# Gated attention feeding a rotation layer: fewer full-float32 chunks, gate sums as matrix products, and a re-planned order

## The chip, the cores and the metric

One NeuronCore of one Trainium2 chip runs the whole kernel. The metric is the device time of one execution in microseconds (us). Lower is better.

## The reference

The inputs are q, k, v and a gate logit, each of 4 batches x 8 heads x 768 tokens x 48, and four weight matrices. What is computed, cut to its core:

```python
f = 1 / (1 + exp(-f_logit))
for t in range(768):
    state = f[t][:, None] * state + outer(k[t], v[t])
    y[t] = q[t] @ state
x = heads side by side                       # 4 x 768 x 384
theta = x @ w_theta
zr, zi = x * cos(theta), x * sin(theta)
u = x + w_tok_r @ zr + w_tok_i @ zi          # over the 768 tokens
out = u + maximum(u @ w_ch, 0)
```

All of it is float32. In this case `w_theta` and `w_tok_i` are drawn about 5.5 times larger than the usual scale, so the angles are large.

## The kernel before, in words

**Chunks.** Each batch is cut into 6 chunks of 128 tokens, 24 chunks in all, numbered m. The recurrence is done chunk by chunk. `gate_clamp` (line 267) bounds the logits below, `gate_open` (271) forms log(1 + exp(-f)) by two ScalarE (ACT) activations, `gate_sum` (277) forms the running sum over the tokens of the chunk as one VectorE (DVE) scan, `gate_exp` (281) takes the exponential of the sum and of its negative, and `gate_q` and `gate_k` (292, 296) multiply q and k with these. `att_scores`, `att_keys`, `att_state`, `att_old` and `att_out` (324 to 402) are the TensorE (PE) products of linear attention within the chunk and with the state, `att_mask`, `att_mid`, `att_new` and `att_fade` their DVE or GpSimd (POOL) steps, and `att_turn` (408) transposes the chunk of x.

**The rotation layer.** `angles` (436) multiplies the chunk with `w_theta`; `whole`, `settle`, `fold` and `trig` reduce the angle and take sine and cosine; `rotate` (468) makes the two products zr and zi. `products` (487) then adds one chunk's share of the token mixing to one block of the output in PSUM: 144 such pieces, named f0, f1 and f2 by the block of 128 channels, 36 for each batch. `channel` (511) is the product with `w_ch`, 3 calls for each half of a batch, and `finish` and `store` end it.

**Two forms of product.** The chunks of batch 0 (`FULL = 1`, in batches) use float32 operands as they are: a piece is two float32 products, and PE runs each as two instructions. All other chunks use operands split in two float32r parts, a high one and a rest, and a piece is six float32r products. The splits are steps of their own: `split_xh`, `split_xl`, `split_zh`, `split_zl` (427 to 482) for the data, `split_hi` and `split_lo` (239, 245) for the weights. The weights arrive as 64-bit numbers in 16 parts and are first decoded (`decode_low`, `decode_high`, `decode_join`, 212 to 226).

**The order.** `ORDER` (72) is one hand-fixed list of steps for all engines. Each step name stands for the next call of its function (`lf` loads the next chunk of f, `gs` is the next `gate_sum`, `sc` the next `att_scores`, `ke` the next transposes of k, and so on); a suffix /D, /P or /A moves the step to DVE, POOL or ACT. Every engine runs its own steps in the order of the list, and each queue is in order, the SP queue that issues all DMAs too. `PLACES` (55) names the buffer that each tile takes. PSUM has two double banks ("a") and four single banks ("b", `bank`, 309) for everything else.

Of the kernel before, what the change touches and what calls it, by code (L numbers as in the profile page):

```python
# [8 lines left out]
F32 = mybir.dt.float32  # L9
# [9 lines left out]
DM = H * D  # L19
# [17 lines left out]
F_MIN = -44.0  # L37
# [6 lines left out]
FULL = 1  # L44
# [3 lines left out]
CUT = 0  # L48
# [7 lines left out]
    "a": "0110110101001010110101010101010101010101010101010",  # L56
    "b": ("012301230120123023300300002121123222230230203120310202001031023333312312023011203100000023"
        "1030303030032123123211120303031"),
    "f": "012012012012012012012012",
# [8 lines left out]
    "wp": "0123456789abcdefghijklmno013245687cd",  # L68
    "x": "012012012012012012012012",
    "z": "0123450123412342342350421350421350421",  # L70
}
ORDER = (
# [39 lines left out]
@with_exitstack  # L112
def gla_moe_kernel(
    ctx: ExitStack,
    tc: tile.TileContext,
    q: bass.AP,
    k: bass.AP,
    f: bass.AP,
    v: bass.AP,
    vt: bass.AP,  # L120
    w_theta: bass.AP,
    w_r: bass.AP,
    w_i: bass.AP,
    w_ch: bass.AP,
# [614 lines left out]
```

## Time and profile before

| what | value |
|---|---|
| time, median of 3 runs | 337.95 us (337.77 to 339.97) |
| the profiled execution | 338.16 us, span 335.5 us |
| PE busy | 316.8 us, 94% of the span |
| DVE busy | 243.4 us, 73% |
| ACT busy | 192.9 us, 58% |
| POOL busy | 112.3 us, 33% |
| table loads on ACT | 22 of 1.28 us |

The span runs from the first to the last instruction that the profiler saw; 2.66 us of the profiled execution lie around it. Busy shares are averages over stages with different limits, so the stages have to be read one by one.

### The profile page before, as it was taken

How to read it: one execution, taken by the hardware profiler on the slowest of the kernel's cores; microseconds unless marked ns; L12 is line 12 of the kernel's file. 1: busy time of each engine (PE TensorE's matmuls, PEld its weight loads, DVE VectorE, ACT ScalarE, POOL GpSimd, SP SyncE). 2: the span in 40 equal slices, each digit the busy share in tenths (PEclk: the TensorE clock that was granted, in tenths of full speed). 3: DMA queues.
4: the chain of work that ended last, by engine and by line, in shares of the span. 5: the costliest groups of instructions: out<-in, count | busy, mean ns of one | idle time of the engine just before them, and what ended most of it. 6: DMA issues, size and time to landing. Idle time of an engine off the chain costs nothing.

```text
span 335.5 us, 9996 instructions
## 1 busy us (share of the span) xinstructions
PE 316.8 (94%) x4320; PEld 280.7 (84%) x4320; DVE 243.4 (73%) x394; ACT 192.9 (58%) x321; POOL 112.3 (33%) x109
## 2 busy tenths in 40 slices
PE   0798999999999999999999999999999999999993
PEld 0685676567676789999999999999999999999992
DVE  5999999999999899968659777774526677441031
ACT  6789977787696799847468253953805342310010
POOL 2452074318100146265371248143800521103110
PEclk9999999999999999999999999999999999999998
DMA  7989779758660463240405353250122102000022
GB/s 266 395 244 304 254 249 340 249 181 308 243 212 17 150 225 111 91 156 15 130 3 168 115 160 117 88 178 0 33 73 79 49 2 73 0 2 0 0 73 77
DMA packets 21619, 45.54 MB, mean 136 GB/s; under 512 B 2369, under 2 KB 5441, under 8 KB 21569
## 3 DMA queue, kind: packets, MB, share of 16 engines
q1 hardware_dynamic: 21568, 44.84, 39.6%
q8 instruction: 36, 0.59, 0.7%
q14 instruction: 15, 0.11, 0.1%
HBM read 40.11 MB, written 4.72 MB: 134 GB/s over the span
## 4 chain that ended last, share of the span: by engine, by line
PE 83%; DVE 9%; ACT 2%; DMA 2%; issue 2%; DVEq 0%; ACTq 0%
PE pm L498 47%; PE pch L516 10%; PE pth L442 9%; PE wide L401 4%; PE wide L393 3%; PE wide L333 3%; PE pxt L411 2%; PE psk L347 2%; PE wide L362 2%; DVE f L279 2%; DMA out_dram<-ut 1%; DVE z L475 1%; DVE raw L215 1%; DMA f<-in_f_dram 1%; DVE k L299 1%
## 5 line engine op out<-in xcount | busy, mean ns | idle before, releaser
L498 PE MATMUL pm<-wp,z 128*128 128x384 f32 x648 | 117.1, 336 | 0.0
L498 PEld LDWEIGHTS pm<-wp,z 128*128 128x128 f32 x648 | 112.4, 188 | 0.0
L498 PE MATMUL pm<-value,z 128*128 128x384 f32 x144 | 49.3, 487 | 0.2 <-DVE z L475 0.2
L516 PE MATMUL pch<-uhl,wch 128*128 128x384 f32 x216 | 40.2, 339 | 0.4 <-DVE ut L176 0.4
L498 PEld LDWEIGHTS pm<-value,z 128*128 128x128 f32 x144 | 26.3, 190 | 15.9 <-DVE value L226 0.5
L516 PEld LDWEIGHTS pch<-uhl,wch 128*128 128x128 f32 x216 | 37.5, 188 | 1.0 <-DVE ut L176 0.7
L290 POOL COPY pes<-p 128x4 f32<-128x4 f32 x24 | 11.4, 476 | 72.6 <-ACT p L286 68.2
L502 DVE TENSOR_TENSOR ut<-pm,ut 128x384 f32<-128x384 f32 x24 | 13.1, 552 | 29.8 <-PE pm L498 29.8
L176 ACT CAST uhl<-ut 128x384 fp32r<-128x384 f32 x18 | 9.2, 509 | 41.5 <-DVE ut L502 41.5
L279 DVE TENSOR_TENSOR_SCAN f<-carry,f 128x512 f32<-128x512 f32 x24 | 29.1, 1222 | 0.7 <-ACT f L275 0.7
L433 POOL TENSOR_TENSOR xl<-ut,xh 128x384 fp32r<-128x384 f32 x13 | 13.5, 1041 | 46.1 <-DVE xh L176 29.1
L286 ACT ACTIVATE p<-f 128x512 f32<-128x512 f32 x24 | 15.1, 628 | 21.7 <-DVE f L279 21.3
L509 POOL TENSOR_TENSOR uhl<-ut,uhl 128x384 fp32r<-128x384 f32 x13 | 13.5, 1047 | 37.0 <-DVE uhl L176 18.6
L347 PE MATMUL psk<-ident,k 128*128 128x128 f32 (+1 forms) x96 | 16.8, 302 | 8.9 <-DVE k L299 8.8
L269 POOL TENSOR_SCALAR f<-f 128x512 f32<-128x512 f32 x14 | 23.3, 1668 | 1.5 <-DMA f<-in_f_dram 1.5
L530 DVE SCALAR_TENSOR_TENSOR ut<-pch,ut 128x384 f32<-128x384 f32 x24 | 13.0, 553 | 14.7 <-PE pch L516 14.4
L482 POOL TENSOR_TENSOR z<-w,z 128x768 fp32r<-128x768 f32 x9 | 17.4, 1931 | 17.8 <-ACT z L176 9.6
L442 PE MATMUL pth<-wth,xh 128*128 128x384 f32 x108 | 23.0, 348 | 0.0
L299 DVE SCALAR_TENSOR_TENSOR k<-f,k 128x512 f32<-128x512 f32 x24 | 19.5, 813 | 3.7 <-ACT f L287 3.6
L401 PEld LDWEIGHTS wide<-v,sc 64*64 64x64 f32 x768 | 15.0, 140 | 8.1 <-issue 4.7
L347 PEld LDWEIGHTS psk<-ident,k 128*128 128x128 f32 (+1 forms) x96 | 11.9, 148 | 11.6 <-POOL pes L290 8.8
L475 DVE TENSOR_TENSOR w<-w,x 128x768 f32<-128x768 f32 x18 | 18.1, 1010 | 4.0 <-ACT w L466 4.0
(84 smaller groups left out, 607.3 us busy)
## 6 DMA issues: line engine op xcount, KB each, us to landing
v<-in_v_dram SPq DMA_DIRECT2D x24, 384.0 KB, 4.4
f<-in_f_dram SPq DMA_DIRECT2D x24, 256.0 KB, 3.6
k<-in_k_dram SPq DMA_DIRECT2D x24, 256.0 KB, 4.1
q<-in_q_dram SPq DMA_DIRECT2D x24, 256.0 KB, 3.9
raw<-in_w_r_dram SPq DMA_DIRECT2D x12, 384.0 KB, 5.1
raw<-in_w_i_dram SPq DMA_DIRECT2D x12, 384.0 KB, 5.6
out_dram<-ut SPq DMA_DIRECT2D x21, 192.0 KB, 2.4
raw<-in_w_theta_dram SPq DMA_DIRECT2D x3, 384.0 KB, 5.5
```

Of the source, the lines that this page charges most:

```text
L269: on(nc.vector).tensor_scalar(ft, ft, F_MIN, None, op0=ALU.max)
L279: nc.vector.tensor_tensor_scan(fl, carry[:, pairs(h)].rearrange("p n t -> p (n t)"), fl, 0.0, ALU.mult, ALU.add)
L286: nc.scalar.activation(ps_[m][:, pairs(h)], ft, AF.Exp, scale=-1.0)
L299: nc.vector.scalar_tensor_tensor(kt, loaded["f", m][:, pairs(h)], E_TOP, kt, op0=ALU.min, op1=ALU.mult)
L347: nc.tensor.transpose(psks[m][:used(m), p, :], loaded["k", m][:, p, :used(m)], ident)
L401: nc.tensor.matmul(out[HALF[t], j, p, :], scs[m][HALF[a], j, p, :], v2[HALF[a], t, p, :], start=(t == 0 and m % NC == 0 and p == 0), stop= ...
L433: on(nc.vector).tensor_tensor(xls[m], src, xhs[m], op=ALU.subtract)
L442: nc.tensor.matmul(pths[m], l, r, start=(n == 0), stop=(n == len(ms) - 1))
L475: nc.vector.tensor_tensor(zs[m] if full else w, w, xs[m].unsqueeze(1).to_broadcast([P, 2, DM]), op=ALU.mult)
L482: on(nc.vector).tensor_tensor(zs[m][:, 0], ws[m], zs[m][:, 1], op=ALU.subtract)
L498: nc.tensor.matmul(pms[g, d], l, r, start=(s == 0 and i == 0), stop=(s == NC - 1 and i == len(ms) - 1))
L516: nc.tensor.matmul(pcs[g, d], l, r, start=(es[0] == 0 and n == 0), stop=(es[-1] == KD - 1 and n == len(ms) - 1))
```

## The change

1. `FULL` counts chunks now. Chunks 0 to 3 stay in float32; chunks 4 and 5 of batch 0 are split like the rest. Of the weight parts, the four that belong to chunks 4 and 5 are split first (`SPLIT`).
2. For the first four chunks (`SUMMED = 4`) the host gives f with tokens on the partitions (`ft`), and `gate_sum` is four float32 PE products of 128 columns with a triangular matrix `upto`, into a PSUM bank; `gate_exp` reads the bank. The scan stays for the other 20 chunks. The sum is no longer negated in place: p and its inverse change places.
3. `gate_clamp` is gone. The first activation of `gate_open` also gives its row sums (`accum_out`, tile `opened`), and `find_worst` tests them near the end with two more DVE instructions; too large a sum leads to the slow recurrence, as a too small product did already.
4. `wu` (`keep_warm`) is a float32 PE product of two constant tiles, 128 x 128 with 128 columns, into a PSUM bank that nobody reads. The order has 30 of them.
5. v is loaded as 3 x 192 columns a chunk in place of 2 x 384. `att_state` and `att_out` read the same 48 columns from other places; the number and the shape of their products stay. The 48 key columns of `att_state` from chunk 2 on (`WHOLE`) are in both kernels.
6. Chunk 0 has its gate steps in two halves (steps that begin with h), and chunk 1 is loaded ahead of it. `ORDER` and `PLACES` are new throughout.

```diff
-FULL = 1
+FULL = 4
-CUT = 0
+CUT = 1
+SUMMED = 4
...
-    "lf gc go lf gc go lf gs lk lq gc gs ge gk gq ke go gp lv sc ge gp gs lk lw lq kt lv lf gk d1 lk lw gq/P lf",
...
+    "wu lf go hlf hlf wu wu wu wu wu wu wu wu hgo hgs lw hlq d1 hgo hgs hge hge d2 hgq/P wu wu gs wu wu hlk hlk",
+    "hgk hgk hlq hgq sc ge wu wu lf go lk d3 di d4 lv ke lq gk wu wu gs kt/D lv up sa st gp sm ge ke wu lf qs",
...
+    "ab/A d1 d2 f1 f2 st tr d3 d3 th gk lw d4/D ge d1 f0 d5 tn se e4 ab/A d2 f1 ro f1 xh/D wu d3 zh f0 v gs lv f2",
+    "e5 lk gk ul/P ul f2 e4 e5 go ke kt zl ou xc sc up gs v v sm/P qs tr ro/P xl c c c ge lk gk gp lq cv uh gq/P",
...
-        if FULL and n < NCH:
+        if n < NTOK or n < NCH and (n - NTOK) % NC < FULL:
...
+    LATE = [n for n in range(NTOK, NCH) if (n - NTOK) % NC >= FULL]
+    SPLIT = [*range(NTOK), *LATE, *[n for n in range(NTOK, NCH) if n not in LATE]]
...
-    def gate_clamp(m, h=None):
-        ft = loaded["f", m][:, pairs(h)]
-        on(nc.vector).tensor_scalar(ft, ft, F_MIN, None, op0=ALU.max)
...
-        nc.scalar.activation(ft, ft, AF.Exp, scale=-1.0)
+        n = B * NC if h else m
+        nc.scalar.activation(ft, ft, AF.Exp, scale=-1.0, accum_out=opened[:, n:n + 1])
...
+        if m < SUMMED:
+            if not h:
+                sums[m] = bank([P, NP, C], f"psum{m}")
+            for p in range(NP)[pairs(h)]:
+                nc.tensor.matmul(sums[m][:, p, :], loaded["f", m][:, p, :], upto, start=True, stop=True)
+            return
...
+        src = sums[m][:, pairs(h)] if m < SUMMED else ft
-        nc.scalar.activation(ps_[m][:, pairs(h)], ft, AF.Exp, scale=-1.0)
-        nc.scalar.activation(ft, ft, AF.Exp)
+        nc.scalar.activation(ps_[m][:, pairs(h)], src, AF.Exp)
+        nc.scalar.activation(ft, src, AF.Exp, scale=-1.0)
...
+    def keep_warm(n):
+
+        nc.tensor.matmul(bank([P, C], f"warm{n}"), ident, carry[:, 1], start=True, stop=True)
...
+        nc.vector.tensor_reduce(worst[:, 1:2], opened, axis=AX.X, op=ALU.max)
...
+            rows = ft[m] if nm == "f" and m < SUMMED else src[m // NC, m % NC]
+            nc.sync.dma_start(loaded[nm, m][:, pairs(h)], rows[:, pairs(h)])
...
-        vs[m] = sb.tile([P, 2, DM], F32, tag="v", bufs=3, name=f"v{m}")
+        vs[m] = sb.tile([P, 3, NP * D], F32, tag="v", bufs=3, name=f"v{m}")
```

How many steps of a kind each list has up to and with the 36th piece of `products` (of 144), counted in the two lists; a half step counts a half:

| engine | step | before | after |
|---|---|---|---|
| PE | pieces in float32 / in float32r | 36 / 0 | 24 / 12 |
| PE | angles in float32 / in float32r | 6 / 3 | 4 / 4 |
| PE | `ke` / `sc` / `up` | 14 / 12 / 13 | 11 / 10 / 11 |
| PE | `qs` / `ou` / `xt` | 12 / 11 / 11 | 10 / 9 / 9 |
| PE | `c` (channel products) | 3 | 0 |
| PE | `gs` as products / `wu` | 0 / 0 | 4 / 28 |
| DVE | clamps / scans | 7 / 15 | 0 / 10 |
| DVE | `gk` / `gq` | 14 / 9 | 13 / 6.5 |
| DVE | `ma`, `sa`, `st`, `sm` | 40 | 34 |
| DVE | `d1` and `d3` | 32 | 32 |
| DVE | splits of weights and data | 12 | 14 |
| DVE | `se`, `ro`, `ab`, `tn`, `v`, `cv`, copies | 29 | 25 |
| POOL | clamps / `d2` | 9 / 5 | 0 / 1 |
| ACT | `d2` | 11 | 15 |

## Rows read from the trace of the kernel before

**Rows 1.** Windows: start:end, length, busy us (instructions) of PE, PEld, DVE, ACT, POOL; PEclk; DMA; GB/s.
```profile
0.00:9.00 9.00, 0.16 (x1) 0.20 (x2) 5.00 (x11) 5.96 (x9) 1.82 (x10) 1.00 0.77 276
9.00:20.00 11.00, 9.58 (x208) 7.98 (x211) 10.38 (x16) 8.38 (x15) 6.71 (x7) 1.00 0.98 351
20.00:39.30 19.30, 17.26 (x384) 12.68 (x376) 18.99 (x31) 17.56 (x33) 4.21 (x7) 1.00 0.85 270
...
0.00:100.00 100.00, 87.58 (x1464) 62.31 (x1465) 93.77 (x144) 80.11 (x135) 36.25 (x44) 1.00 0.79 272
100.00:124.70 24.70, 24.70 (x334) 18.86 (x333) 23.43 (x40) 18.70 (x31) 4.66 (x5) 1.00 0.40 131
124.70:329.80 205.10, 204.49 (x2525) 199.58 (x2524) 125.72 (x211) 94.11 (x157) 71.37 (x61) 1.00 0.22 71
329.80:335.50 5.70, 0.00 (x0) 0.00 (x0) 0.53 (x2) 0.00 (x0) 0.00 (x0) 0.76 0.32 112
```

**Rows 2.** Waits of PE: who waited for whom, total us, times, longest.
```profile
PE psk L347 <- DVE k L299: 8.8, 1, 8.8
PE wide L401 <- DVE sc L339: 1.4, 2, 0.9
```

**Rows 3.** Timeline of PE, 0 to 45 us: start, duration, what.
```profile
8.84 1.08 PE L347 MATMUL psk<-ident,k 128*128 128x128 f32 x4 [8.84 <-DVE k L299]
...
23.64 1.11 PE L347 MATMUL psk<-ident,k 128*128 128x128 f32 x4
...
31.50 0.60 PE L347 MATMUL psk<-ident,k 128*128 128x128 f32 x4
```

**Rows 4.** The chain that ended last, in order of time: start, duration, what.
```profile
0.81 2.80 DMA f<-in_f_dram
...
61.77 1.94 PE pth L442 x6
...
67.57 0.65 PE wide L401 x32
68.22 0.59 PE psk L347 x4
...
70.71 0.48 PE wide L333 x32
71.55 0.48 PE pxt L411 x3
...
123.40 1.29 PE pm L498 x4
124.69 1.56 PE pth L442 x9
...
133.39 4.19 PE pm L498 x24
```

**Rows 5.** Groups by line and shape: count, busy us, mean ns, idle before.
```profile
L279 DVE TENSOR_TENSOR_SCAN f<-carry,f 128x512 f32<-128x512 f32 x24 | 29.1, 1222 | 0.7 <-ACT f L275 0.7
...
L269 POOL TENSOR_SCALAR f<-f 128x512 f32<-128x512 f32 x14 | 23.3, 1668 | 1.5 <-DMA f<-in_f_dram 1.5
...
L299 DVE SCALAR_TENSOR_TENSOR k<-f,k 128x512 f32<-128x512 f32 x24 | 19.5, 813 | 3.7 <-ACT f L287 3.6
...
L274 ACT ACTIVATE f<-f 128x512 f32<-128x512 f32 x24 | 15.1, 628 | 2.5 <-DVE f L269 2.0 <-POOL f L269 0.3
...
L294 DVE TENSOR_TENSOR q<-q,p 128x512 f32<-128x512 f32 x15 | 12.9, 861 | 0.0
...
L269 DVE TENSOR_SCALAR f<-f 128x512 f32<-128x512 f32 x10 | 4.1, 414 | 2.2 <-DMA f<-in_f_dram 2.2
```

**Rows 6.** Timelines of POOL and DVE, 0 to 45 us.
```profile
11.29 1.27 POOL L294 TENSOR_TENSOR q<-q,p 128x512 f32<-128x512 f32 x1 [0.88 <-DMA q<-in_q_dram]
...
11.32 1.66 DVE L215 TENSOR_SCALAR raw<-raw 128x768 int32<-128x768 int32 x1
...
31.68 0.55 DVE L215 TENSOR_SCALAR raw<-raw 128x768 int32<-128x768 int32 x1
```

More of the change, by code (lines that the diff above doesn't have):

```diff
@@ L219, in decode_high @@
         low, high = words(n)
-        nc.scalar.activation(high.bitcast(F32), high.bitcast(F32), AF.Copy, scale=2.0 ** -112)
+        if on(nc.scalar) is nc.scalar:
+            nc.scalar.activation(high.bitcast(F32), high.bitcast(F32), AF.Copy, scale=2.0 ** -112)
+        else:
+            on(nc.scalar).tensor_scalar(high.bitcast(F32), high.bitcast(F32), 2.0 ** -112, None, op0=ALU.mult)
     def decode_join(n):
@@ L237, in place @@
         return parts[n][2][i]
+    LATE = [n for n in range(NTOK, NCH) if (n - NTOK) % NC >= FULL]
+    SPLIT = [*range(NTOK), *LATE, *[n for n in range(NTOK, NCH) if n not in LATE]]
     def split_hi(n):
-        if parts[n][1] and not FULL:
-            nc.scalar.mul(place(n, 1), values[n], parts[n][1])
-        else:
-            copy(nc.scalar, place(n, 1), values[n])
+        copy(nc.scalar, place(n, 1), values[n])
     def split_lo(n):
-        if parts[n][1] and not FULL:
-            nc.vector.scalar_tensor_tensor(place(n, 0), values[n], parts[n][1], place(n, 1),
-                                           op0=ALU.mult, op1=ALU.subtract)
-        else:
-            on(nc.vector).tensor_tensor(place(n, 0), values[n], place(n, 1), op=ALU.subtract)
+        on(nc.vector).tensor_tensor(place(n, 0), values[n], place(n, 1), op=ALU.subtract)
     tables = []
@@ L362, in att_state @@
                     nc.tensor.matmul(out[r, t, p, :], kts[m][HALF[t], p, r],
[L363 removed]
+                                     vs[m][HALF[t], j, p * D:(p + 1) * D], start=True, stop=True)
     def att_mid(m):
@@ L474, in rotate @@
                 zs[m], zs[m + 1] = two[:, 0], two[:, 1]
-        nc.vector.tensor_tensor(zs[m] if full else w, w, xs[m].unsqueeze(1).to_broadcast([P, 2, DM]), op=ALU.mult)
+        on(nc.vector).tensor_tensor(zs[m] if full else w, w, xs[m].unsqueeze(1).to_broadcast([P, 2, DM]), op=ALU.mult)
     def split_zh(m):
@@ L564, in inner, with later @@
         return lambda n: fn(n // (NC - 1) * NC + n % (NC - 1))
-    def later(fn, per, first=FULL):
-        return lambda n: fn(n + first * per)
+    def later(fn, first):
+        return lambda n: fn(n + first)
     def piece(d):
@@ L574, in go @@
             b = g // NTH
-            products(g, s, d, zs[b * NC + s], b < FULL)
+            products(g, s, d, zs[b * NC + s], b * NC + s < FULL)
         return go
@@ L595, in gla_moe_kernel @@
         "st": inner(att_new), "sm": inner(att_fade), "qs": att_old, "ou": att_out, "xc": att_x, "xt": att_turn, "xs": keep_x,
[L596 to L598 removed]
+        "xh": later(lambda m: split_xh(m, u_slice(m)), FULL), "xl": later(lambda m: split_xl(m, u_slice(m)), FULL),
+        "th": lambda m: angles(m, m < FULL), "tn": whole, "se": settle, "ab": fold, "tr": trig,
+        "ro": lambda m: rotate(m, m < FULL), "zh": later(split_zh, FULL), "zl": later(split_zl, FULL),
         "f0": piece(0), "f1": piece(1), "f2": piece(2), "v": group(add_u), "uh": group(split_uh), "ul": group(split_ul), "c": channels, "cv": group(finish),
[L600 removed]
+        "so": group(lambda g, d: store(g // NTH, g, d)), "fl": find_worst, "wu": keep_warm,
     }
@@ L699, in rows @@
         return np.ascontiguousarray(t.transpose(0, 3, 2, 1, 4))
+    f = rows(inputs["f_logit"])
     v = np.asarray(inputs["v"])
@@ L704, in layout @@
     halves = v.transpose(0, 2, 1, 3).reshape(B, NC, 2, HF, NP, 2, D)
-    rolled = np.stack([np.stack([halves[:, :, t, :, :, a ^ t] for t in range(2)], axis=3) for a in range(2)], axis=2)
-    v2 = np.stack([halves.reshape(B, NC, C, DM), rolled.reshape(B, NC, C, DM)], axis=3)
-    v2 = np.ascontiguousarray(v2)
+    parts = [halves[..., 0, :], halves[..., 1, :], halves[:, :, ::-1, :, :, 1, :]]
+    v2 = np.ascontiguousarray(np.stack([a.reshape(B, NC, C, NP * D) for a in parts], axis=3))
     return {
@@ L710, in layout @@
         "k": rows(inputs["k"]),
-        "f": rows(inputs["f_logit"]),
+        "f": f,
+        "ft": np.ascontiguousarray(f.reshape(B * NC, P, NP, C)[:SUMMED].transpose(0, 3, 2, 1)),
         "v": v2,
```

57 lines of the change are left out of this document (29 added, 28 removed), and 67 rows, old and new, of the table ORDER.

## The prediction

> **What bounds the kernel now.** I read the windows first. PE is busy for 0.16 us of the first 9, 9.6 of the next 11, 17.3 of the next 19.3, and without a gap from 39.3 us on: up to 100 us it adds 60.6 us in 60.7, from 100 to 124.7 us 24.7 in 24.7, and 204.5 in the 205.1 behind that [rows 1]. DVE is the other way round: 10.4 of 11 us and 19.0 of 19.3 us in the two stretches in which PE has gaps, still 23.4 of 24.7 up to 124.7 us, and only 125.7 of 205.1 afterwards [rows 1]. So the kernel starts on DVE and the gate chain, and from 39.3 us PE sets the end. The waits of PE say the same: 8.8 us for the first `gate_k`, then 1.4 us in two waits for the mask, and nothing else above 0.6 us [rows 2].
>
> The timeline of PE shows a second loss. The four transposes of a chunk take 1.08 us at 8.84 us, still 1.11 us at 23.64 us, and 0.60 us at 31.50 us [rows 3], though the granted clock reads 1.00 in every window up to 124.7 us [rows 1]. By the durations, PE works at its lower level, 1.2 GHz, until about 25 us, after nearly 9 us of idleness and through several gaps, and at 2.4 GHz from then on. The windows are no witness for this, the durations are.
>
> The 36th piece (the last of batch 0, with which float32 products end) ends in the chain at 124.7 us [rows 4], and 210.8 us follow, 5.7 of them a tail without PE [rows 1]. I use this piece as the meeting point: what each engine must do ahead of it is counted in the table of the change.
>
> **The change, part by part.**
>
> *Less float32.* A float32 piece takes 1.29 us of the chain, four float32r pieces 4.19, so 1.05 each; a float32 angle product 1.94, a float32r one 1.56 [rows 4]. Twelve pieces and two angle products change form: 12 x 0.24 + 2 x 0.38 = 3.7 us less for PE. The two chunks' splits cost other engines some 2 x 3.3 us, spread over POOL, ACT and DVE; the DVE share is in the count below.
>
> *Gate sums on PE, and `wu`.* No row shows a float32 product of 128 columns. Lower bound: an angle product streams 384 columns in 0.323 us an instruction [rows 4], a third of it is 0.108. Upper bound at full clock: the transposes, 0.59 for four [rows 4], 0.148 an instruction; at the lower level 0.27 [rows 3]. A gain is excluded, as work is added. I take 0.148, as it is the row with the same weight load. A product is two instructions, 0.30 us: 16 gate products cost 4.7 us, 30 `wu` 8.9 us. Together this is more than float32r gives back, so PE has more work after the change: what counts is whether it lies where PE idles now. All gate products and 28 `wu` stand ahead of the 36th piece, the other two `wu` behind the last product, where only DVE's last step and a store follow; they cost nothing.
>
> *The start.* Today the first f lands at 3.61 us [rows 4]. After: chunk 1 opens from there to 4.9 (two activations of 0.63 [rows 5]); the halves of chunk 0, about 0.33 an activation by the same row, to 6.3; the gate products of the second half to 6.9 at the low clock; its two exponentials to 8.2; then `gate_k` and `gate_q` of half size to about 9.1. k and q come later in SP's queue than now, behind two weight loads; with some 4 us of issues ahead of them and the 2.8 us that the first f took to land [rows 4] or more, I expect them between 7 and 9 us, an estimate. So the first scores are at about 9.4 us, against 9.9 now (behind the first transposes [rows 3]). Little is won before this point, but PE will have done 13 `wu` and half of the gate products (6.3 us of work) by then, and DVE only 1.6 us.
>
> *Up to the 36th piece, PE.* By the table and the chain's prices (pieces and angles as above, transposes 0.55, scores and `up` and `qs` and `xt` 0.5, `ou` 0.65, `c` 1.56 [rows 4]) the list holds 105.6 us before and 102.0 after, 13.2 of it new work. From 9.9 us, with 6.8 done, PE alone would get there at 9.9 + 95.2 = 105.1 us.
>
> *Up to the 36th piece, DVE.* It was busy for 117.2 us up to 124.7 [rows 1]. Less: 5 scans x 1.22, 7 clamps x 0.41, one `gk` 0.81, 2.5 `gq` x 0.86 [rows 5], six mask and state steps 2.9 and four other steps 2.0 (0.3 to 0.7 each, estimates from the neighbouring rows by size); more: two splits, 1.9. That is 6.1 + 2.9 + 0.8 + 2.2 + 2.9 + 2.0 - 1.9 = 15.0 less, 102.2 us. From 9.4 us, with 1.6 done, DVE alone gets there at 9.4 + 100.6 = 110.0 us. So DVE is late next: it replaces PE's idleness as the limit of this stage. Two reasons make it less than 110.0. Its last listed steps (a weight split, a `gate_k`, half of a `ul`, about 2 us) feed nothing in the 36th piece. And POOL, which loses nine clamps of 1.67 us [rows 5] and four decodes in this stage, disturbs DVE less: a decode step on DVE took 1.66 us beside a POOL multiply and 0.55 alone [rows 6]. I take 1 us for that, one such collision.
>
> The Trainium skill, "SBUF — State Buffer", section "SBUF: two separate sides", says that VectorE and GpSimd share a port pair as an exclusive lock: whichever starts first holds it for its whole instruction and the other is blocked. The trace agrees: the multiply ends at 12.56 us and the 1.66 us step at 12.98. By the rule each of the nine clamps could have blocked DVE by up to its length, and the relief would be 3 to 5 us rather than 1, which would bring the end 2 to 4 us earlier, towards the second rival.
>
> *ACT* has about 100 us listed ahead of the piece against 103 before, four more decodes and three fewer gate openings among it, and begins at 3.6 us; it is not the limit. The row sums are bounded by nothing and, as an instruction of their own like the shortest activation, 0.5 us: 14 of these would be 7 us, ending ACT near 110, level with DVE. I take nothing, since the activation passes over these elements anyway.
>
> *The rest.* Clamps removed from POOL, half-size loads, a smaller v and the two extra steps of the final test lie beside PE work; if their cover went, each is below 1 us. The 48 columns of `att_state` change nothing, since both kernels have them.
>
> *The sum.* The 36th piece ends at 110.0 - 2.0 - 1.0 = 107.0 us. Behind it the new list holds more than the old one, since fewer chunks are done by then: three `ke`, two each of `sc`, `up`, `qs`, `ou`, `xt`, one angle product and three `c`, which is 1.65 + 5.2 + 1.56 + 4.7 = 13.1 us. So the span is 107.0 + 210.8 + 13.1 = 330.9 us, and with the 2.66 us around it 333.6. The profiled execution, 338.16, lies 0.2 above the median of the runs: I predict 333.4 us, 1.3% faster. No change would need the 36th piece at 111.6 us.
>
> **The rivals.**
>
> *DVE keeps its full price.* The steps listed last do count and POOL's relief doesn't show, and each wait between DVE and PE adds: piece 36 at 110 to 113 us, span 333.9 to 336.9, time 336.4 to 339.4: no change that can be told (about 1% is what a measurement here can tell). For it: DVE is at 95 to 98% in this stage now, with no slack [rows 1], and behind the piece the new list keeps DVE level with PE for another 30 us. Against: PE has not waited for DVE from 39.3 to 124.7 us, though DVE was as full [rows 1].
>
> *PE alone is the limit.* DVE runs ahead, piece 36 at 105.1 us: span 329.0, time 331.5. For it: `wu` keeps PE at the higher level from early on, and DVE loses its clamps and scans at the very start. Against: DVE's own count.
>
> *The clock stays low (the slower side).* The place is PE from its first `wu`, at about 1.6 us, to a time t; up to t it does half of its work. Then piece 36 ends at t + 102.0 - (t - 1.6)/2 = 102.8 + t/2. At t = 25, as now [rows 3], that is 115.3 us, span 339.2, time 341.7, 1.1% slower: the added 13 us then lie on the path. It decides from t = 17.6 on. For it: the new list has waits in the same places (first k, first mask) and does more on PE there. Against: the `wu` stand in just these places, and today PE reached the higher level at 25 us even with gaps of half a microsecond close before.
>
> The Trainium skill, "TensorE: Matmul & The Clock Gate", section "What's actually happening", says that the low clock is the default and sustained activity releases it. The trace agrees as far as it goes, with 1.11 us against 0.60 for the same four transposes; by that rule t would be below 10 us, and this rival falls.
>
> **How the numbers follow.** Forecast 0.50, DVE at full price 0.28, PE alone 0.10, low clock 0.12. Of the forecast, 0.46 lies beyond 1% faster and 0.04 within; of DVE at full price 0.26 within and 0.02 slower; PE alone is faster; the low clock slower. Faster by over 1%: 0.56; within 1%: 0.30; slower: 0.14. The range reaches from below PE alone, with the added products nearer their lower price (two microseconds less), 329.5, to the upper end of DVE at full price, 339.4.
>
> **What would show it.** Right: the transposes of the first chunks take 0.60 us well ahead of 25 us; the first scores at 9 to 10 us; the 36th piece ends between 105 and 109 us; PE's waits are for DVE (mask, `gate_k`, z), a few us in all between 10 and 107 us; PE's busy time is near 320 us. Wrong: gaps of PE between 60 and 107 us that sum to over 4 us (DVE at full price); transposes of 1.1 us beyond 17 us (clock); float32r pieces of chunks 4 and 5 waiting for their weight splits; `wu` or gate products over 0.30 us each at full clock, or ACT idle nowhere up to 100 us (row sums).

## The result, and the profile after

The changed kernel takes 342.4 us (median of 4 runs, 341.29 to 343.49) against 337.86 for the kernel before beside it: ratio 1.0142 (95% interval 1.0105 to 1.0179). It is slower by 1.4%, where 1.3% faster was forecast; the time lies above the range. The profiled execution took 343.49 us, the longest of the four, with a span of 341.0. One run each of `x3_no_warm`, `y1_no_warm_early` and `w3_short_decode` below was slower than its fellows by over 1.5%; medians and ratios leave it out, and the one profile of `w3_short_decode` is of such a run.

First the windows of the changed kernel, in the stretches of [rows 1] as far as the 36th piece.

```profile
0.00:9.00 9.00, 6.99 (x42) 6.59 (x42) 0.98 (x5) 5.90 (x15) 1.69 (x12) 1.00 0.73 215
9.00:20.00 11.00, 9.63 (x200) 8.36 (x202) 9.26 (x20) 9.17 (x19) 4.44 (x6) 1.00 0.97 342
20.00:39.30 19.30, 15.12 (x387) 11.07 (x386) 13.17 (x20) 13.45 (x25) 6.96 (x8) 0.91 0.70 234
39.30:60.00 20.70, 19.73 (x348) 14.19 (x349) 20.38 (x33) 19.44 (x36) 6.95 (x7) 1.00 0.87 291
...
100.00:124.70 24.70, 24.70 (x328) 22.04 (x331) 23.59 (x38) 22.18 (x36) 10.77 (x10) 1.00 0.38 118
```

The start does what it should: PE has done 7 us of work by 9 us, and DVE is busy for 1.0 us there (5.0 before) and for 9.3 of the next 11 (10.4 before). The third line is wrong for every part of the forecast: between 20 and 39.3 us PE is busy for 15.1 us (17.3 before), DVE for 13.2 (19.0), ACT for 13.5 (17.6). For a part of it, from 29.2 to 31.9 us, all engines stand still together, and the granted clock is 0.91 of the full one over the stretch. The waits of PE name the place:

```profile
PE wide L373 <- issue: 3.9, 1, 3.9
PE warm L551 <- POOL causal L163: 1.7, 1, 1.7
PE wide L345 <- POOL pes L305: 1.0, 1, 1.0
```

One wait of 3.9 us is put down to "issue": no semaphore that the profile shows ended it. The timeline of PE (start, us, line, operation, count, idle time before) shows where it falls:

```profile
22.72 2.20 PE L454 MATMUL pth<-value,ut 128*128 128x384 f32 x6
...
27.41 0.55 PE L373 MATMUL wide<-v,ktok 64*48 64x48 f32 x31
31.87 0.24 PE L373 MATMUL wide<-v,ktok 64*48 64x48 f32 x1 [3.91 <-issue]
32.05 0.55 PE L423 MATMUL pxt<-ident,x 128*128 128x128 f32 x3
32.43 0.91 PE L359 MATMUL psk<-ident,k 128*128 128x128 f32 x4
33.27 1.14 PE L412 MATMUL wide<-v,sc 64*64 64x48 f32 x32
34.34 3.00 PE L454 MATMUL pth<-value,ut 128*128 128x384 f32 x6
```

PE stops before the last of 32 equal products of one `att_state` call, all with the same two operand tiles. It is not an operand that comes late. Behind the stop the same angle product takes 3.00 us instead of 2.20 and four transposes 0.91 instead of 0.63 (at 25.03 us): the clock has fallen to its lower level, 1.2 GHz. The window of the stop shows that, and the window before it how full the DMA engines were:

```profile
9.85:27.96 18.11, 17.24 (x432) 14.22 (x432) 16.12 (x30) 16.10 (x33) 6.49 (x8) 1.00 0.90 311
27.96:36.00 8.04, 4.13 (x43) 3.04 (x44) 3.61 (x7) 3.92 (x7) 2.13 (x4) 0.79 0.47 155
```

What can come late without a semaphore is the instructions themselves. The page of the profile lists a DMA queue of its own for them, beside the one for data:

```profile
q1 hardware_dynamic: 22000, 42.48, 37.7%
q8 instruction: 37, 0.61, 0.8%
```

These are 37 packets of 16 KB. In the trace's records of the packets the third runs from 29.49 to 30.42 us, and PE goes on at 31.87. Counted over all of PE's instructions in the kernel (weight loads, products and the short ones that wait for a semaphore), the one that PE waits for is its 961st. The 36th piece ends at 113.8 us in the chain (last line here), where 107.0 was forecast and 124.7 was measured before [rows 4].

```profile
4.57 5.28 DMA q<-in_q_dram
...
27.96 3.91 issue
...
107.33 3.13 PE pm L510 x18
110.68 3.13 PE pm L510 x18
```

Behind it follow 227.2 us against 223.9 forecast. The chain ends with the two last `wu`:

```profile
329.87 3.47 PE pch L528 x20
333.34 0.23 PE warm L551 x2
333.57 0.04 issue
333.62 0.49 PE warm L551 x2
```

### The profile page after: what moved, and what is told of

Same layout as the page of the kernel before. It is cut to its first block, busy times and chain, and to the rows that moved or that the text cites. A ratio compares the mean times of both kernels' runs of the same rounds, so it can differ in the third digit from the quotient of the medians.

```text
span 341.0 us, 10311 instructions
## 1 busy us (share of the span) xinstructions
PE 324.6 (95%) x4442; PEld 294.1 (86%) x4442; DVE 240.7 (71%) x393; ACT 196.0 (57%) x343; POOL 107.1 (31%) x107
## 4 chain that ended last, share of the span: by engine, by line
PE 80%; DVE 8%; DMA 3%; issue 3%; ACT 2%; SPq 1%; DVEq 0%; ACTq 0%
PE pm L510 41%; PE pth L454 11%; PE pch L528 9%; PE wide L412 4%; PE wide L404 3%; PE wide L345 3%; PE psk L359 3%; PE pxt L423 2%; PE wide L373 2%; DMA out_dram<-ut 2%; DMA q<-in_q_dram 2%; PE warm L551 1%; DVE k L314 1%; DVE sc L351 1%; DVE ut L542 1%
## 5 line engine op out<-in xcount | busy, mean ns | idle before, releaser
L510 PE MATMUL pm<-wp,z 128*128 128x384 f32 x720 | 133.1, 338 | 0.0
L510 PE MATMUL pm<-value,z 128*128 128x384 f32 x96 | 33.1, 488 | 0.0
L487 POOL TENSOR_TENSOR w<-w,x 128x768 f32<-128x768 f32 x10 | 19.8, 1982 | 39.1 <-ACT w L478 33.4
L305 POOL COPY pes<-f 128x4 f32<-128x4 f32 x24 | 13.4, 558 | 39.0 <-ACT f L302 26.9
L542 DVE SCALAR_TENSOR_TENSOR ut<-pch,ut 128x384 f32<-128x384 f32 x24 | 12.9, 550 | 12.6 <-PE pch L528 12.4
L351 DVE TENSOR_TENSOR sc<-wide,causal 128x512 f32<-128x512 f32 x24 | 16.3, 680 | 7.7 <-PE wide L373 7.6
L454 PEld LDWEIGHTS pth<-wth,xh 128*128 128x128 f32 x120 | 20.6, 188 | 1.4 <-ACT ktok L183 0.3
L314 DVE SCALAR_TENSOR_TENSOR k<-p,k 128x512 f32<-128x512 f32 (+1 forms) x25 | 21.3, 854 | 0.3 <-ACT p L301 0.2
L309 POOL TENSOR_TENSOR q<-q,f 128x512 f32<-128x512 f32 (+1 forms) x11 | 14.6, 1328 | 13.3 <-DMA q<-in_q_dram 12.3
L345 PE MATMUL wide<-q,k 48*64 48x64 f32 x768 | 16.8, 221 | 1.4 <-POOL pes L305 1.0
L412 PE MATMUL wide<-v,sc 64*64 64x48 f32 x768 | 17.6, 227 | 0.5 <-DVE sc L351 0.4
```

Source lines behind the costliest of these rows:

```text
L309: on(nc.vector).tensor_tensor(qt, qt, loaded["f", m][:, pairs(h)], op=ALU.mult)
L314: nc.vector.scalar_tensor_tensor(kt, ps_[m][:, pairs(h)], E_TOP, kt, op0=ALU.min, op1=ALU.mult)
L345: nc.tensor.matmul(out[HALF[j ^ t], j, p, :], kt[r, p, HALF[t]], qt[r, p, HALF[t]], start=True, stop=True)
L351: nc.vector.tensor_tensor(scs[m], scores_of(m), mask, op=ALU.mult)
L412: nc.tensor.matmul(out[HALF[t], j, p, :], scs[m][HALF[a], j, p, :], vs[m][HALF[a], 2 * j, p * D:(p + 1) * D], start=(t == 0 and m % NC == ...
L454: nc.tensor.matmul(pths[m], l, r, start=(n == 0), stop=(n == len(ms) - 1))
```

## The experiments

All ratios are to the kernel before, timed on the same chip in the same batch; its medians in these lie between 337.31 and 337.64 us, so a difference between kernels of two batches carries some 0.3 us. The last columns of the tables come from the one profile of each kernel: when the 36th piece ends, and for how long PE was busy and idle up to there. In the kernel before it was busy for 112.3 us and idle for 12.4. Two theories were on the table first: PE's instructions come late, because more of them are needed earlier while the DMA engines are full; or the added products simply cost their time, or the clock.

**One load elsewhere, and the warm-up products away.** The first kernel moves one weight load ahead in the list, from behind a `gs` (about 23 us) to behind a `lv` (about 16 us), so that the DMA engines are less full when the third packet is wanted. The second leaves out the two last `wu`, the third all 30. The fourth puts 22 `wu` at the head of the kernel before.

```diff
# x1_early_load (ORDER)
-... lv lq sc tn gk gs lw qs ...
+... lv lw ... lv lq sc tn gk gs qs ...
# x2_no_tail_warm (28, 29), x3_no_warm (0 to 29): keep_warm(n); the places of all other tiles stay
+        if n in (28, 29):
+            return
# x4_before_warm (ORDER of the kernel before)
-    "lf gc go lf gc go ...
+    "wu wu wu ... (22 of them) lf gc go lf gc go ...
```

> The changed kernel with the fourth weight load (w_r and w_i of one part, 768 KB) moved forward in SP's order, from about 23.3 us to right behind the v load at 15.8 us; no engine's work changes. Theory A (PE ran out of instructions at 28 us: its 16 KB instruction packet, asked for near 22.5 us, stood behind the data loads until 29.5 us): 2.3 us of data leave the backlog in front of that packet, the gap of PE shrinks from 3.9 us to 1.6 or goes, the clock stays up, and the time falls by 2.3 to 5.5 us from 342.4, to 337 to 340. Rival B (the gap is a wait of PE for data or for another engine that the profile misnames): the gap stays at 3.5 to 4 us and the time within 0.7 us of 342.4.

> The changed kernel without the last two constant products, which stand behind the last channel product. Theory: PE's last branch, which ends the span, waits for them; it comes 0.5 to 1.0 us earlier and the time falls by as much, to about 341.6. Rival (as in the prediction: they lie beside DVE's last step and the store): no change, 342.4. The gap of 3.9 us near 28 us stays under both.

> The changed kernel without any of the 30 constant products. Theory A (late instruction packet): PE has 104 instructions fewer ahead of the same place, reaches the end of its loaded instructions later, the gap of 3.9 us shrinks to under 2 us; PE's clock goes up later than 5.3 us, which costs little as long as DVE sets the pace: 338 to 341. Rival C (the clock of the first 25 us is what the constant products buy): transposes take 1.1 us until beyond 20 us and the time rises to 344 or more. Rival D (the constant products themselves lie on the path): the time falls by up to their 8.4 us, to 334 to 336.

> The kernel before with 22 constant products at the head of its list, in the 8.8 us in which PE has nothing, and nothing else. If DVE sets the pace of the first 39 us: the transposes take 0.60 us from the start, and the time is within 1 us of before's 337.9. If the low clock cost PE's time there: 3 to 6 us faster, 332 to 335. Theory A adds: 88 more PE instructions and a faster PE bring the instruction packet near 30 us under pressure; a gap named issue of 1 to 3 us may appear near 28 to 32 us, and then the time is at or above before's.

| kernel | us, median | ratio (95%) | 36th piece ends | PE busy / idle to there |
|---|---|---|---|---|
| after | 342.40 | 1.0142 (1.0105 to 1.0179) | 113.8 | 105.2 / 8.7 |
| x1_early_load | 339.08 | 1.0043 (1.0026 to 1.0060) | 110.7 | 105.0 / 5.7 |
| x2_no_tail_warm | 340.36 | 1.0076 (1.0056 to 1.0095) | 113.3 | 105.0 / 8.3 |
| x3_no_warm | 336.72 | 0.9977 (0.9943 to 1.0010) | 110.6 | 98.3 / 12.2 |
| x4_before_warm | 337.47 | 0.9991 (0.9969 to 1.0013) | 124.7 | 116.9 / 7.8 |

Moving one load, with every product kept, gives back 1% of the time: two thirds of the loss. PE's wait in that kernel:

```profile
PE wide L374 <- issue: 0.8, 1, 0.8
```

It is the same instruction, the 961st, 0.8 us late instead of 3.9. Up to the 36th piece PE's busy time is the same in both kernels, and the idle time is 3.0 us less. The windows of `after` and of `x1_early_load`, first up to that piece and then from PE's 705th instruction to the end of the third packet, show this, and that the DMA engines were full in one of them and nearly free in the other (0.97 and 0.08, the last figure but one):

```profile
0.00:113.81 113.81, 105.15 (x1621) 81.64 (x1622) 97.05 (x154) 93.73 (x170) 31.77 (x43) 0.99 0.68 229
0.00:110.65 110.65, 104.97 (x1621) 82.28 (x1622) 96.29 (x154) 93.81 (x170) 30.18 (x43) 0.98 0.71 236
25.39:30.42 5.03, 2.45 (x130) 2.02 (x128) 2.65 (x5) 3.30 (x7) 2.89 (x3) 1.00 0.97 340
27.94:30.03 2.09, 1.97 (x104) 1.67 (x105) 2.09 (x4) 1.90 (x5) 1.20 (x2) 1.00 0.08 26
```

Without any `wu` the loss is gone (0.9977), more than the theory of late instructions asked for and just less than the rival that puts the whole price on the `wu`. Taking off the two last `wu` gave more than either expectation. On the kernel before, 22 `wu` at the head change nothing either way: they fill time in which PE idles there, and the higher clock, which they bring from 6.4 us on with two falls before 27 us, ends the 36th piece no earlier in that order.

**Time or number.** What is it about the `wu`, the time that they hold PE or their being instructions? `y2_tiny_warm` keeps all 30 but gives each one column instead of 128; `w1_few_long` keeps the first 13 and puts four of 512 columns (16 instructions) where fifteen of 128 stood; `y4_start_warm` keeps the first 13 alone, and `y1_no_warm_early` has none and the early load as well.

```diff
# y2_tiny_warm
-        nc.tensor.matmul(bank([P, C], f"warm{n}"), ident, carry[:, 1], start=True, stop=True)
+        nc.tensor.matmul(bank([P, C], f"warm{n}")[:, :1], ident, carry[:, 1, :1], start=True, stop=True)
# y4_start_warm
+        if n in range(13, 30):
+            return
# w1_few_long: n < 13 as they were, then four of
+            nc.tensor.matmul(bank([P, NP * C], f"warm{n}"), ident, carry.rearrange("p n t -> p (n t)"), start=True, stop=True)
```

> The changed kernel without the 30 constant products and with the fourth weight load moved forward to 15.7 us. Theory A (late instruction packets behind a full DMA backlog): the remaining gap of 2.2 us near 34.5 us of the run without constant products shrinks with the backlog or moves to another boundary; if it goes, 333 to 335, if it only moves, 336 to 337.5. Rival (that gap is a wait for a mask or a bank): it stays at 2 us at the same place and the time at 336.9.

> The changed kernel with all 30 constant products cut to 1 column in place of 128: the same number of PE instructions at the same places, about a third of their PE time. Theory A (it is the number of instructions ahead of the packet): the gap near 28 us stays at 2 us or more and the time at 340 to 342. Rival (their PE time is what costs): the time falls to that of the run without them, 336 to 338, with no gap near 28 us. If what they do for the clock mattered, the transposes at 11 to 17 us take 1.1 us.

> The changed kernel with the first 13 constant products alone, those ahead of the first scores. Theory A: 52 PE instructions more than without any, half of what the changed kernel has: a gap near 28 to 32 us between 0 and 2.5 us, time 336.5 to 339.5. If only the 13 to 15 between the first scores and 21 us do the harm: as without any, 336 to 337.5, or better by what an early clock gives.

> The run with 13 constant products, plus four constant products of 512 columns in the stretch from the first scores to 21 us, where the changed kernel has 15 of 128 columns: about as much PE time (some 3.4 us against 4), 16 PE instructions in place of 60. Theory A (the number of instructions ahead of the late packet is the cost): time 336.0 to 338.5, near the 336.5 without them. Rival (their PE time is the cost): 339 or more, towards 340.4, the changed kernel without its last two.

| kernel | us, median | ratio (95%) | 36th piece ends | PE busy / idle to there |
|---|---|---|---|---|
| y1_no_warm_early | 336.78 | 0.9980 (0.9954 to 1.0005) | 110.2 | 100.3 / 9.9 |
| y2_tiny_warm | 345.09 | 1.0231 (1.0167 to 1.0294) | 115.3 | 111.0 / 4.3 |
| y4_start_warm | 336.50 | 0.9974 (0.9946 to 1.0002) | 109.5 | 101.6 / 7.9 |
| w1_few_long | 338.12 | 1.0020 (0.9996 to 1.0044) | 109.8 | 104.1 / 5.6 |

`y2_tiny_warm` can't tell the two apart, and its 345.09 us were outside both expectations (340 to 342, 336 to 338). A `wu` of one column holds PE for as long as one of 128: the first 18 instructions take 3.97 us, against 3.93 in `after`. And the clock came up later: its record shows the upper level from 19.0 us only, and the lower one again from 32.66 to 39.48, as the transposes at 17.72 us confirm (1.11 us, the sign that its expectation named for the clock). PE is busy for 5.9 us more up to the 36th piece than in `after`, and idle for 4.4 us less. What this run shows is above all the price of the lower clock.

```profile
1.74 3.97 PE L551 MATMUL warm<-carry,ident 128*128 128x1 f32 x18 [1.74 <-POOL causal L163]
17.72 1.11 PE L359 MATMUL psk<-ident,k 128*128 128x128 f32 x4
```

`w1_few_long` does tell them apart. Its four long products hold PE for 4.4 us, about as much as the fifteen, but are 16 instructions in place of 60. It takes 1.6 us more than `y4_start_warm` (338.12 - 336.50), and the fifteen take 3.9 (340.36 - 336.50, with `x2_no_tail_warm`, which has them without the last two); the intervals of the two ratios, 1.0020 and 1.0076, don't meet. So these products cost more than their PE time, and their number has a part in it: the 25 `wu` ahead of the stop are 100 instructions.

The trace's packet records say how. Here are stops of PE with the packet that comes before each (us):

```
kernel             packet       PE stops, goes on   at instruction  packet's end to PE's start
after              29.49-30.42  27.76 - 31.87        961            1.45
x1_early_load      28.86-30.03  30.31 - 31.36        961            1.33
x2_no_tail_warm    28.93-29.86  28.12 - 31.16        961            1.30
y2_tiny_warm       30.45-31.48  30.71 - 32.78        961            1.30
x3_no_warm         33.17-35.54  34.47 - 36.90       1217            1.36
y1_no_warm_early   35.26-36.19  36.62 - 37.60       1217            1.41
w1_few_long        33.81-34.74  34.41 - 36.06       1217            1.32
```

The stops stand at instruction 961 or 1217, 256 apart, which is what a packet of 16 KB holds at 64 bytes an instruction. PE goes on 1.3 to 1.5 us after the packet's end. In all 19 profiles, with or without a stop, none of the instructions 449, 705, 961 and 1217 starts sooner than 1.3 us after the end of its packet, the first to the fourth. This and the move of one load are what shows the cause; that a wait without a semaphore stands there would not.

The records show one thing more: in no profile does one of these four packets begin before PE is within 13 instructions of the start of the 256 ahead of it. So it matters less how early PE comes to instruction 961 than how fast it runs through the block before. In `after` it takes 2.4 us from 705 to 960, most of them products of 48 or 64 columns and their weight loads; the third packet begins 4.1 us after 705 (0.9 in `x1_early_load`) and takes 0.9 us. In the kernel before, the same 256 take 6.5 us, and PE doesn't stop. Each of the 13 profiles of the new order with gate products has one block that PE runs through in 2.4 to 3.3 us, and PE waits for a packet behind each of these, for 0.2 to 4 us. Removing the `wu` doesn't end the stops: it moves the fast block to 961 to 1216, and the stop with it, to 1217.

**Is it the start, the queue, or more data?** Three changes to `y4_start_warm`: the first weight load goes behind the k and q of chunk 0 (`z1_first_loads`), `accum_out` goes, and with it the test of the sums (`z2_no_row_sums`), and four copies of 384 KB within DRAM go beside the weight loads (`z3_more_loads`).

```diff
# z1_first_loads (ORDER)
-... hgs lw hlq d1 hgo hgs hge hge d2 ... hlk hlk hgk hgk hlq hgq sc ge ...
+... hgs hlq hgo hgs hge hge ... hlk hlk hgk hgk hlq lw hgq sc ge d1 d2 ...
# z2_no_row_sums
-        nc.scalar.activation(ft, ft, AF.Exp, scale=-1.0, accum_out=opened[:, n:n + 1])
+        nc.scalar.activation(ft, ft, AF.Exp, scale=-1.0)
# z3_more_loads, four times
+        nc.sync.dma_start(extra[n], w_r[n * P:(n + 1) * P, :TH].bitcast(I32))
```

> The run with 13 constant products (336.5 us), with the first weight load behind the k and q loads of chunk 0 in SP's order and its first decode steps (d1 on DVE, d2 on ACT) behind the first gate multiplies. Theory E (the start is late because the first k and q stand behind 768 KB of weights, and d1 stands on DVE ahead of the first gate_k and waits for these weights to 8.8 us): first scores at 8.8 to 9.3 us in place of 10.35, the 36th piece 0.8 to 1.4 us earlier than 109.5, time 335.0 to 335.8. Rival (the weights are needed as early as they come, or the data loads as a whole set the pace to 40 us): first scores earlier, but the 36th piece and the time within 0.4 us of the run it starts from.

> The run with 13 constant products, without the row sums of the first gate activation (the tile for them is set to zero; the test for too large sums is left out). Each row sum is an instruction of 0.19 us on ACT behind its activation, 25 in all. If ACT is on the path up to the 36th piece: 1 to 2.5 us faster, 334 to 335.5. If ACT has slack there: within 0.5 us of 336.5.

> The run with 13 constant products, with four copies of 384 KB from DRAM to DRAM added in SP's queue, one behind each of the third to sixth weight loads; nothing waits for them. Theory F (the DMA engines, at 0.9 to 1.0 from 9 to 40 us, set the pace there and delay the instruction packets): each copy costs about 1 us, the 36th piece ends 2 to 5 us later, PE shows gaps named issue, time 338.5 to 341.5. Rival (DVE and ACT set the pace; loads are hidden): within 0.7 us of 336.5.

| kernel | us, median | ratio (95%) | 36th piece ends | PE busy / idle to there |
|---|---|---|---|---|
| z1_first_loads | 340.12 | 1.0059 (1.0030 to 1.0089) | 113.3 | 105.4 / 7.9 |
| z2_no_row_sums | 337.96 | 1.0004 (0.9975 to 1.0033) | 107.8 | 100.3 / 7.5 |
| z3_more_loads | 337.98 | 0.9989 (0.9962 to 1.0016) | 110.7 | 104.5 / 6.2 |

None of the three came out as either of its expectations. The first brings the first scores from 10.35 us to 9.17 and loses 3.6 us (340.12 - 336.50). PE stops at instruction 961 again, from 32.14 to 33.85, but its idle time up to the 36th piece is that of `y4_start_warm` (7.9 us); it is its busy time that is 3.8 us longer, with the granted clock at the lower level from 13.71 to 23.95 us and from 34.19 to 37.60 (in `y4_start_warm` from 22.24 to 25.65). Why the clock fell there is not shown. The second tells nothing: the intervals of the two overlap, though the one profile of it, the only one of this group without a fall of the clock, is the best up to the 36th piece. The copies cost 1.5 us, within the spread of these kernels (their runs reach from about 335.5 to 339.5). PE stopped at 961 from 31.27 to 33.28, the direction of the theory, but it idled less than in `y4_start_warm`, and 2.8 us more of busy time go with a lower clock from 12.63 to 22.87 us.

**Was DVE the limit?** The forecast rested on DVE. `w2_pool_gq` moves six full `gate_q` steps from DVE to POOL; `w3_short_decode` leaves out the first instruction of `decode_join`, so that the low bits of the weights are missing, and takes about 14 us from DVE.

```diff
# w2_pool_gq (ORDER, six places)
-... gq ...
+... gq/P ...
# w3_short_decode
-        nc.vector.scalar_tensor_tensor(low, high, 3, low, op0=ALU.logical_shift_left, op1=ALU.bitwise_or)
```

> The run with 13 constant products, with the six gate multiplies of q that DVE does up to the 36th piece moved to POOL, which is busy for about a quarter of that stage. Theory G (with the instruction gap nearly gone, DVE's own work sets the 36th piece, at 110 us): DVE loses about 4 to 5 us, the piece ends 2 to 4 us earlier than 109.5, time 333 to 335. Rival (POOL's 1.45 us a step and what it takes from DVE give it back, or loads set the pace): the time within 0.8 us of 336.5.

> The run with 13 constant products, with the first of the two join instructions of every weight decode left out (the weights lose the low bits that it joins): 16 DVE instructions of 0.5 to 0.95 us, 14 us of DVE work up to the 36th piece, and nothing else. Theory G (DVE sets the 36th piece): it ends 4 us or more earlier, at 105 or below, time 330 to 333. Rival H (loads, late instruction packets and the low clock set it): at most 1.5 us earlier, 335 to 336.5.

The first measured 337.35 us (0.9995, 0.9965 to 1.0025), the second 334.78 (0.9923, 0.9902 to 0.9943). Against `y4_start_warm` that is +0.85 and -1.7 us. 14 us less for DVE buy 1.7: its work is not what ends this stage. The windows of `w2_pool_gq` say why the busy share misled:

```profile
0.00:39.30 39.30, 32.55 (x640) 25.80 (x640) 26.21 (x49) 32.38 (x65) 17.52 (x28) 0.96 0.84 271
39.30:100.00 60.70, 60.31 (x904) 44.22 (x904) 59.85 (x86) 52.63 (x92) 21.32 (x22) 1.00 0.74 252
```

From 39.3 us on PE has hardly a gap (60.3 of 60.7 us) although DVE is as full as before; ahead of 39.3 us DVE has 13 us to spare.

**The gate sums, in both orders.** `y3_no_warm_scan` is the changed kernel without `wu` and with DVE scans in place of the products. The last three go the other way: the kernel before with the clamp replaced by row sums alone (`v1_before_no_clamp`), with gate sums as products alone (`v2_before_sums`), and with both (`v3_before_both`).

```diff
# y3_no_warm_scan (and no wu)
-        src = sums[m][:, pairs(h)] if m < SUMMED else ft
+        src = ft
# v1_before_no_clamp, v3_before_both
-    "lf gc go lf gc go lf gs ...
+    "lf go lf go lf gs ...
-        nc.scalar.activation(ft, ft, AF.Exp, scale=-1.0)
+        nc.scalar.activation(ft, ft, AF.Exp, scale=-1.0, accum_out=opened[:, m:m + 1])
# v2_before_sums, v3_before_both, gate_sum
+        if m < SUMMED:
+            for p in range(NP):
+                nc.tensor.matmul(sums[m][:, p, :], loaded["f", m][:, p, :], upto, start=True, stop=True)
+            return
```

> The changed kernel without constant products and with the gate sums of chunks 0 to 3 back as DVE scans (f of these chunks loaded with channels on the partitions again). If DVE sets the pace up to the 36th piece, four scans of 1.2 us more on DVE end that piece 3 to 5 us later and the time is 340 to 342; if the wait for instructions and the loads set it, the time stays within 1 us of 336.9, and 64 PE instructions fewer make the gaps named issue smaller.

> The kernel before, with part 3 of the change alone: no clamp, row sums in the first gate activation, and the longer test at the end; the order is otherwise that of before. If the gate chain's first steps set the start: the first transposes come 0.4 us earlier and the time falls by 0.4 to 1.5 us, to 336 to 337.1. If other engines' waits take it up, or the row sums on ACT (0.19 us each) give it back: within 0.4 us of before.

> The kernel before, with part 2 of the change alone: the gate sums of chunks 0 to 3 as PE products with the triangular matrix, four PSUM banks taken between its own, f of these chunks loaded with tokens on the partitions. DVE loses four scans of 1.22 us in the first 25 us, PE gains 32 instruction pairs where it idles. If DVE's place in the chain sets the start (as the scans put back in the changed kernel, 3.9 us slower, say): 2 to 4 us faster, 333.5 to 335.5. If late instruction packets and loads set it: within 1 us of before, with a gap named issue near 28 to 32 us.

> The kernel before with parts 2 and 3 together, in the order of before. If they add up: 3 to 5 us faster than before, 332.5 to 334.5. If the start is set by loads and instruction packets: within 1 us of before.

| kernel | us, median | ratio (95%) | 36th piece ends | PE busy / idle to there |
|---|---|---|---|---|
| y3_no_warm_scan | 340.77 | 1.0104 (1.0053 to 1.0154) | 114.0 | 97.0 / 17.0 |
| v1_before_no_clamp | 336.98 | 0.9981 (0.9959 to 1.0002) | 123.8 | 111.9 / 11.9 |
| v2_before_sums | 340.81 | 1.0102 (1.0061 to 1.0144) | 129.2 | 116.1 / 13.0 |
| v3_before_both | 340.24 | 1.0076 (1.0051 to 1.0102) | 128.4 | 113.6 / 14.8 |

In the new order the products are worth 4 us (340.77 - 336.72): with scans PE waits 11.5 us for the first `gate_k`. That is what this run's DVE theory forecast (340 to 342), and at the start DVE is in the chain that PE waits for; but it is the chain's length and not DVE's load, as DVE is busy for only 27.7 of the first 39.3 us there. In the old order the same products cost 3.3 us (340.81 - 337.53), and the two runs that have them missed both their expectations. PE waits there for ACT, but in `v2_before_sums` it idles hardly longer than before up to the 36th piece (13.0 us against 12.4): its busy time is what grew, from 112.3 to 116.1 us, as the 32 instructions take 7.7 us of PE and bring it no earlier start (10.44 us for the first scores, 9.85 before). The waits of PE, of `y3_no_warm_scan` and then of `v2_before_sums`:

```profile
PE wide L341 <- DVE k L310: 11.5, 1, 11.5
PE wide L369 <- DVE ktok L183: 3.5, 1, 3.5
```

```profile
PE psum L294 <- ACT f L283: 5.4, 1, 5.4
PE psum L294 <- ACT ktok L184: 1.9, 1, 1.9
```

Dropping the clamp alone brings about what its DVE time says: PE's first wait is 8.2 us instead of 8.8 [rows 2], the 36th piece ends 0.9 us earlier, and the median is 0.55 us lower, with an interval that just reaches no change.

## Why the prediction was wrong

**The step that failed** is "it replaces PE's idleness as the limit of this stage", said of DVE, and with it the sum "110.0 - 2.0 - 1.0 = 107.0 us". PE's idleness was not replaced, it came back for another reason: a wait of 3.9 us for instructions, and the fall of the clock behind it. I counted PE's work in time and never in instructions. A `wu` or a gate product is two instructions, each with its weight load: the 25 `wu` and 16 gate products ahead of the stop are 164 instructions that the kernel before doesn't have there, and at the upper clock PE comes to its 961st at 27.8 us instead of 34.7, having run through the 256 before it in 2.4 us instead of 6.5. Its instructions come in a queue beside the loads that the change put in a new order.

Point by point:

- *The 36th piece at 107.0 us.* It ended at 113.8, 6.8 late. The stop accounts for 3.9. The lower clock behind it is on record from 32.57 to 35.98 us; at half speed that is 1.7. The first scores came at 10.16 us instead of 9.4, because q landed 5.28 us after its issue (first line of the chain): 0.8. These make 6.4, measured from a sum that was itself wrong (next point). By PE's own count it was busy for 105.2 us, where the forecast had 102.0 (102.7 by its prices as printed), and idle for 8.7, where the forecast for PE alone left 3.1.
- *DVE's 110.0 us.* `x3_no_warm`, `y1_no_warm_early` and `y4_start_warm` end the piece at 109.5 to 110.6 us, close to this number, but that is luck: `w3_short_decode` shows that DVE's price is not what ends it. The sum had 102.2 us of work for DVE, without a pause from 9.4 us on; in `after` DVE worked 97.1 us up to the piece and stood idle for 7.9 of the 30.3 us between 9 and 39.3. What is left in `y4_start_warm` is PE's loss ahead of 39.3 us (7.7 of its 7.9 us of idle time), and its waits that are put down to DVE sum to 0.9 us. My argument against the second rival, "DVE's own count", was thus no argument.
- *Two tail `wu`, "they cost nothing".* They stand between the last product and the end: 333.34 to 334.11 us in the chain, 0.8 us. Without them the time is 2.0 us lower (342.40 - 340.36); a part of that is a stop that was 2.8 instead of 3.9 us in that profile. The rest of the tail, from PE's last product to the end of the span, is 6.84 us (340.95 - 334.11) against 5.74 before (335.46 - 329.72). No experiment took that 1.1 apart; in `x1_early_load`, which has the same two `wu`, this rest is 6.09.
- *Behind the piece.* 13.1 us more were forecast and 16.4 came (227.2 - 210.8): 0.8 for the tail `wu`, 1.1 for the tail behind them, and 1.4 that I did not trace.
- *The price of the added products.* 0.30 us was too much at full clock: eight instructions of gate sums take 0.89 us and six of `wu` 0.67 in the chain, 0.22 a product. At the lower clock, up to 5.3 us, 18 `wu` instructions take 3.93 us, 0.44 a product.

```profile
17.22 0.67 PE warm L551 x6
17.89 0.89 PE psum L290 x8
```

- *Row sums for nothing.* They are an instruction of their own on ACT, `ACTIVATION_READ_ACCUMULATOR`, 25 of 188 ns, 4.7 us in all. That lies within the bound of 0.5 us each. The reason for taking nothing, that the activation passes over these elements anyway, had no row behind it; whether they cost time is not shown, as `z2_no_row_sums` was not told from `y4_start_warm`.

```profile
L280 ACT ACTIVATION_READ_ACCUMULATOR f<-f 128x1 f32 x25 | 4.7, 188 | 0.0
```

**What held.** Float32r gives what was counted: 18 instructions, three pieces, take 3.13 us in the chain, 1.04 each. The start is near what was drawn: half of the gate sums before 9 us, scores at 10.16. The clock is at its upper level far earlier, from 5.3 us on. PE has hardly a gap from 39.3 us on (1.0 us up to 60). And without the `wu` the change is not slower.

**The rivals.** The slower one, "the clock stays low", gave 341.7 us, nearest in number, and its mechanism is not what happened: the clock was up at 5 us and fell only after PE had stopped. (`y2_tiny_warm` is nearer to this rival.) The Trainium skill was right there ("TensorE: Matmul & The Clock Gate", "What's actually happening"): sustained activity raised it, idleness let it fall; the `wu` from 1.74 us on were followed by the upper level at 5.3, the stop from 27.96 on by the fall at 32.57. The port rule of the Trainium skill ("SBUF — State Buffer", "SBUF: two separate sides") was to bring a gain beyond the forecast. It decided nothing, as DVE's work was not the limit; the page also holds it only for certain VectorE instructions (those in a 2-port mode, or with two inputs from SBUF), a condition that the prediction left out. The page of the Trainium skill that bore on this case I had not weighed: "Runtime: NRT & Kernel Launch", section "Instruction fetch mechanics", says that instructions come in 16 KiB blocks of 256 through a DMA queue that the sequencer drives, the next one while the current one runs, and that this is mostly hidden. The trace agrees with the blocks (37 packets, 0.61 MB; stops 256 apart) and their order (none of the first four begins before PE is within 13 instructions of the block ahead of it) and not with the hiding: 3.9 us here, 0.8 with one load moved.

**What stays open.** It is not shown why a packet begins as late as it does. Full DMA engines go with it in `after` and free ones with the short wait in `x1_early_load`, but they don't set its length: in the kernel before the third packet begins 2.1 us after PE's 705th instruction at a share of 0.95, and `z3_more_loads` moved the time by less than its spread. The profiles also differ in when the granted clock fell, for 3.4 to 10.2 us at a time ahead of 40 us or not at all. It may be these two that make the runs of one kernel differ by 4 us (`y4_start_warm` from 335.11 to 339.19), where the kernel before went from 336.55 to 339.11 in the same batch; that was not tested. And why the changed kernel without its late `wu` gains next to nothing where 4.5 us were forecast is only located, in PE's idle time ahead of 39.3 us. Of the complete kernels that were run, `y4_start_warm` (336.50), `x3_no_warm` (336.72), `y1_no_warm_early` (336.78) and `v1_before_no_clamp` (336.98) are the fastest; none is told from the kernel before.

## What to carry to other kernels

Count the instructions of an engine as well as their time, and look for the stretch in which it runs through 256 of them fastest. The last 17 of the products that only keep PE warm cost 1.7% here (0.9974 against 1.0142), the greater part of it ahead of the 36th piece, where PE came to the end of its loaded instructions while the DMA engines were full of data; the two at the very end lie bare in the tail. A wait put down to "issue" in the middle of a run of equal instructions is the sign; compare it with the instruction queue's packets, and move a load before removing work. An engine at 95% beside an idle bottleneck is a candidate, not a limit: take work off it in one experiment before building a forecast on it.

## What was not expected of the hardware

- Instructions of PE arrive in packets of 16 KB on a DMA queue of their own, most of the first four taking 0.9 to 1.3 us, and PE starts on one 1.3 us after its end at the earliest. None of these begins before PE is within 13 instructions of the 256 ahead of it, so 256 instructions in 2.4 us were enough for a stop. In `after` it was 3.9 us, and every engine stood still with PE.
- After a stop of 3.9 us the granted clock fell to its lower level for 3.4 us, with PE at work again at 31.87 us and the fall recorded at 32.57.
- A product of one column held PE as long as one of 128: 18 instructions, with their weight loads, in 3.97 and 3.93 us.
- The same edit (gate sums as products) is worth 4 us in one order and costs 3.3 in the other.
